# Strided attention scores for two batches in one product, and an attention stage ordered by a list scheduler

## The chip, the core and the metric

The kernel runs on one core of a Trainium2 chip. A core has a matrix engine (TensorE: PE in the profile, its weight loads PEld), a vector engine (VectorE, DVE), a scalar engine (ScalarE, ACT), GpSimd (POOL) and SyncE (SP), which here issues all transfers between HBM and SBUF. Each engine works through its own instructions in their order; a wait holds back all that stands behind it on that engine. The metric is the device time in microseconds (us), lower is better.

## The reference

Three layers, all in 32-bit floats, B = 4 batches, 8 heads, S = 576 positions, D = 64.

```python
# attention: heads 0-3 local (a window of 32), heads 4-7 strided (same position mod 32)
scores = (q @ k.T) / sqrt(64)
mask_local   = (rel >= 0) & (rel < 32)            # rel = query position - key position
mask_strided = (rel >= 0) & (key % 32 == query % 32)
attn = softmax(where(mask, scores, -1e9));  x = attn @ v     # x: 2304 tokens x 512
# soft mixture of experts: 32 slots, 8 experts of 512 x 1024 x 512
logits = x @ phi;  d = softmax(logits, axis=tokens);  c = softmax(logits, axis=slots)
slot_out[e] = relu((d.T @ x)[e] @ w1[e]) @ w2[e];  y = c @ slot_out
# MLP: 512 -> 2048 -> 512 on 2304 tokens
out = elu(y @ w_in) @ w_out
```

## The kernel before, in words

**Stages.** Attention with the pooled slot input runs until about 106 us of the profiled execution, the experts (w1, then w2) until about 142 us, and the last MLP takes the rest. Nearly all input passes through one queue on SP: q, k and v (16 MB), w1 and w2 (16.8 MB each) and the MLP's weights. SBUF is full, so that most weight loads go into regions that an earlier stage has to give up first: the dictionary `LOADS` (lines 424 to 436) issues them after given units.

**Units.** Attention is cut into 20 units (line 39, `ORDER`, L for local, S for strided): a pair of heads and a sixth of the positions of the local pairs (12 units), or a quarter of the residues of the strided pairs (8 units). The strided positions are sorted by residue mod 32, so that one residue has 18 positions (`MR`). One unit passes through these steps:

- `emit_A` (line 165). Local: a mask product (line 172) and 12 products of 32 queries of one batch with 128 key columns (line 180). Strided: a mask product (line 190) and 32 products of 18 queries of one batch with the 18 keys of each of the pair's two heads, 36 columns (line 194); the four batches write four bands of 32 partitions. Each 32-bit product is two passes with a weight load each in the trace. Then on DVE the row maximum (line 205) and the subtraction (line 206), both straight from PSUM.
- `emit_E` (line 212): exp on ACT.
- `emit_N` (line 216): on DVE sum (223), + 1e-9 (224), reciprocal (225), the product with it (229) and a 32x32 transpose (233). `spread` copies the four 32-row bands into a block-diagonal tile `bd`, of which there are two: local units two on ACT and two on GpSimd (lines 241, 243), strided units all four on ACT.
- `emit_PV` (line 253): the product with v (lines 262, 276) and its copy to `x_all` by ACT (lines 267, 281).
- `emit_X` (line 287), after a third of a pair's positions: the product with phi (291), six transposes (298), their copies by ACT (308), the sum into `logits` on DVE (301, 303). There are 12 of these.

**Order.** It is written out by hand in the loop of lines 442 to 457. Iteration `it` issues on DVE the first four steps of unit it-1, then maximum and subtraction of unit it, then the transpose of unit it-1; on PE the scores of unit it, then the product with v of unit it-2, then the `emit_X` that `X_AT` names; on ACT exp of unit it, the spreads of unit it-1, the copies of unit it-2 and those of `emit_X`. The tail (lines 504 to 530) is written out too: the pooled sums `acc` of the three thirds are put between the last units' steps.

```python
    for it in range(nu):
        m = it - 2
        na = emit_N(it - 1) if 0 <= it - 1 < nu else []
        aa = emit_A(it) if it < nu else []
        for f in na[0:4] + aa + na[4:]:
            f()
        emit_E(it)
        for f in pend_S:
            f()
        if 0 <= m < nu:
            emit_PV(m)
        for x in X_AT.get(it, ()):
            emit_X(*x)
        for f in LOADS.get(it, ()):
            f() if callable(f) else f[0](*f[1:])
```

Before the loop, GpSimd builds the masks and clears tiles (lines 314 to 358): the padded key tiles kA and kB, `bd` and `pst`. The experts' stage (lines 577 to 706) and the MLP, whose operations a list scheduler puts in order (lines 985 to 1036), are the same in both kernels.

Of the kernel before, what the change touches and what calls it, by code (L numbers as in the profile page):

```python
# [19 lines left out]
def attn_moe_mlp(ctx, tc, q, k, v_l, v_s, phi, w1, w2, w_in, w_out, out):  # L20
# [18 lines left out]
    ORDER = "LLSLSSLSSLSSLSLLLLLL"  # L39
# [35 lines left out]

    def slot(i, name):
# [21 lines left out]
    smask = misc.tile([128, 1, MR], F32, name="smask")  # L98
# [26 lines left out]
    v2_sb, v3_sb = region("v2", "v2"), region("v3", "v3")  # L125
    VT = {2: v2_sb, 3: v3_sb, 0: v0_sb[:, 0:QW], 1: v0_sb[:, QW:2 * QW]}
# [21 lines left out]
    pend_S = []  # L148

# [7 lines left out]
    nth = [sum(y[0] // 2 == x[0] // 2 for y in units[:n]) for n, x in enumerate(units)]  # L157
    st = {}

# [5 lines left out]
    def emit_A(n):  # L165
        p, t, h = units[n]
        qt, kt = qk_t[p]
        if p < 2:
            u = 2 * t + h
            ps = s_ps[n % 2][:, 0:384].rearrange("p (a b) -> p a b", b=64)  # L170
            m0 = 0 if u == 0 else 1
            nc.tensor.matmul(
                s_ps[n % 2][:, 0:384], ident16, lmask16[:, m0:m0 + 3].rearrange("p i h x -> p (i h x)"),
                start=True, stop=False,
            )
            for j in range(3):
                i = 3 * u + j
                for b in range(B):
                    c0 = 128 * i + 32 * b
                    nc.tensor.matmul(  # L180
                        ps[32 * b:32 * b + 32, 2 * j:2 * j + 2, :], qt[:, c0:c0 + 32], kpair(p, i, b),
                        start=False, stop=(j == 2),
                    )
            s = small("s", 384, "ls", 3, 6, 64)
            ops_ = []
            w = 6
            pa = s
        else:
            ps = s_ps[n % 2][:, 0:16 * MR].rearrange("p (a b) -> p a b", b=MR)
            nc.tensor.matmul(s_ps[n % 2][:, 0:16 * MR], ident16, smask16, start=True, stop=False)  # L190
            for j in range(0, 16, 2):
                for b in range(B):
                    c0 = 576 * h + 288 * (j // 8) + B * MR * (j % 8 // 2) + b * MR
                    nc.tensor.matmul(
                        ps[32 * b:32 * b + MR, j:j + 2, :], qt[:, 1152 * t + c0:1152 * t + c0 + MR], kt[:, t, :, c0:c0 + MR],
                        start=False, stop=(j == 14),
                    )
            s = small("s", 16 * MR, "ss", 3, 16, MR)
            ops_ = []
            w = 16  # L200
            pa = pst[nth[n] % 2][:, :, 0:MR]
        sh = [128, w, s.shape[2]]
        mx = sl_p.tile([128, 16, 1], F32, tag="mx", name="mx", bufs=3)
        sc = ps
        ops_.append(lambda: nc.vector.reduce_max(out=mx[:, 0:w, 0], in_=sc, axis=AX.X))  # L205
        ops_.append(lambda: nc.vector.tensor_tensor(  # L206
            out=s, in0=sc, in1=mx[:, 0:w].to_broadcast(sh), op=ALU.subtract
        ))
        st[n] = [pa, w, sh, s]
        return ops_  # L210

    def emit_E(n):
        pa, s = st[n][0], st[n].pop()
        nc.scalar.activation(out=pa, in_=s, func=AF.Exp, scale=scale)

    def emit_N(n):
        p, t, h = units[n]
        pa, w, sh = st[n]
        sm = sl_p.tile([128, 16, 1], F32, tag="sm", name="sm", bufs=4)
        st[n].append(sm)  # L220
        sv = sm[:, 0:w]
        ops_ = [
            lambda: nc.vector.reduce_sum(out=sv[:, :, 0], in_=pa, axis=AX.X),
            lambda: nc.vector.tensor_scalar(out=sv, in0=sv, scalar1=1e-9, scalar2=None, op0=ALU.add),
            lambda: nc.vector.reciprocal(out=sv, in_=sv),
        ]
        bd = bds[n % 2]
        st[n].append(bd)
        ops_.append(lambda: nc.vector.tensor_tensor(out=pa, in0=pa, in1=sv.to_broadcast(sh), op=ALU.mult))
        r, x = (12, 32) if p < 2 else (16, MR)  # L230
        tr = small("pt", 32 * r, "tr", 2, r, 32)
        pin = pa.rearrange("p a (k x) -> p (a k) x", x=32) if p < 2 else pst[nth[n] % 2]
        ops_.append(lambda: nc.vector.transpose(out=tr, in_=pin))  # L233

        def spread():
            for b in range(B):
                q32 = slice(32 * b, 32 * b + 32)
                o, i = bd[q32, 0:r, 32 * b:32 * b + x], tr[q32, :, 0:x]
                e = SPREAD[1 if p >= 2 else 2 if n == nu - 1 else 0][b]
                if e == "A":  # L240
                    nc.scalar.activation(out=o, in_=i, func=AF.Copy)  # L241
                elif e == "G":
                    nc.gpsimd.tensor_copy(out=o, in_=i)  # L243
                else:
                    nc.vector.tensor_copy(out=o, in_=i)

        pend_S.append(spread)
        return ops_

    SPREAD = ("GAGA", "AAAA", "GAVA")  # L250
    nu = len(units)

    def emit_PV(n):
        p, t, h = units[n]
        pa, w, sh, sm, pt = st.pop(n)
        if p < 2:
            o = o_ps[nth[n] % 2][:, 0:384].rearrange("p (j x) -> p j x", x=128)
            for j in range(3):
                i = 3 * (2 * t + h) + j
                for k in range(2):  # L260
                    for e in range(2):
                        nc.tensor.matmul(  # L262
                            o[64 * e:64 * e + 64, j, :], v_t[p][:, max(i - 1 + k, 0), e, :], pt[:, 4 * j + 2 * e + k],
                            start=(k == 0), stop=(k == 1),
                        )
            i = 3 * (2 * t + h)
            nc.scalar.activation(out=x_all[:, POS[p], i:i + 3, :], in_=o, func=AF.Copy)
        else:
            xv = x_all[:, POS[p]].rearrange("p m (b q) -> p q b m", b=B)
            for g in range(2):  # L270
                og = ps_t.tile([128, 512], F32, tag="t", name="so")[:, 0:4 * B * MR]
                for j in range(4):
                    c0 = B * MR * j
                    r = 4 * g + j
                    for hh in range(2):
                        nc.tensor.matmul(
                            og[64 * hh:64 * hh + 64, c0:c0 + B * MR], v_t[p][:, t, h, hh, r, :],
                            pt[:, 8 * hh + r].rearrange("p (b m) -> p b m", b=B)[:, :, 0:MR], start=True, stop=True,
                        )
                q0 = 16 * t + 8 * h + 4 * g  # L280
                nc.scalar.activation(
                    out=xv[:, q0:q0 + 4], in_=og.rearrange("p (j b m) -> p j b m", b=B, m=MR), func=AF.Copy
                )

    seen = set()

    def emit_X(p, t):
        xt = x_all[:, POS[p], 6 * t:6 * t + 6, :]
        lg = ps_l.tile([128, 192], F32, tag="l", name="lg")
        for b in range(B):  # L290
            nc.tensor.matmul(
                lg[32 * b:32 * b + 32, :], phi_sb[:, p, :], xt[:, :, 32 * b:32 * b + 32], start=True, stop=True
            )
        xps = []
        for g in range(2):
            xps.append(ps_t.tile([128, 3, 128], F32, tag="t", name="xtps"))
            for j in range(3):
                nc.tensor.transpose(xps[g][:, j, :], xt[:, 3 * g + j, :], ident)  # L298
        d = logits[:, 192 * t:192 * t + 192]
        if t not in seen:  # L300
            nc.vector.tensor_copy(out=d, in_=lg)
        else:
            nc.vector.tensor_tensor(out=d, in0=lg, in1=d, op=ALU.add)
        seen.add(t)
        if p == 1:
            nc.vector.reduce_max(out=nm3[:, t:t + 1], in_=d, axis=AX.X)
        for g in range(2):
            nc.scalar.activation(out=xt[:, 3 * g:3 * g + 3], in_=xps[g], func=AF.Copy)

    with tc.manual_schedule():  # L310
# [15 lines left out]
        for b in range(B):  # L326
# [115 lines left out]
        for it in range(nu):  # L442
# [6 lines left out]
            for f in pend_S:  # L449
                f()  # L450
# [636 lines left out]
```

## Time and profile before

| | us |
|---|---|
| median of 3 runs (lowest to highest) | 375.57 (374.45 to 375.98) |
| the profiled execution's own time | 374.55 |
| its span, first to last instruction | 372.8 |
| PE, DVE, ACT, POOL busy | 344.3, 262.7, 246.0, 25.9 |

The profile shows one execution. Its views are the page (shares of each engine, 40 slices of the span with the granted PE clock and the rate of the transfers), groups of instructions, waits (what an idle engine waited for), the chain of waits that ended last, stretches of time, and a timeline.

### The profile page before, as it was taken

To read this page: it belongs to the slowest core of one execution; us is meant where nothing else is said; L and a number is where in the kernel's file an instruction comes from. 1 tells how busy PE (TensorE), PEld (TensorE's weight loads), DVE (VectorE), ACT (ScalarE), POOL (GpSimd) and SP (SyncE) were. 2 spreads that over 40 slices of the span, in tenths; PEclk is the share of its full clock that TensorE was granted. 3 is DMA by queue.
4 is the path that set the end of the run, shared out by engine and by line. 5 is a ranking of instruction groups with operands and counts; after the bars stand their busy time and mean duration, and the time that the engine had idled before them with its cause. 6 is when DMAs were issued, how large, how long until landed. Compare 5 with 4: busy or idle time off the path is not lost.

```text
span 372.8 us, 7425 instructions
## 1 busy us (share of the span) xinstructions
PE 344.3 (92%) x2957; PEld 252.9 (68%) x2957; DVE 262.7 (70%) x535; ACT 246.0 (66%) x482; POOL 25.9 (7%) x60
## 2 busy tenths in 40 slices
PE   7576797798799999999999999999999999999995
PEld 4464565576333337878688778888868888888884
DVE  6778648689261317979999999999854665476741
ACT  5469569767423226999999678868665666666660
POOL 8611011122020000000000000000000000000000
PEclk9699889999999999999999999999999999999999
DMA  7999998996899999755000144100000011033301
GB/s 223 389 414 415 421 419 293 401 413 219 329 413 396 421 408 405 280 225 193 34 1 0 41 186 183 44 1 0 2 0 1 2 56 56 2 113 113 114 0 56
DMA packets 15970, 71.58 MB, mean 192 GB/s; under 512 B 1600, under 2 KB 1856, under 8 KB 11328
## 3 DMA queue, kind: packets, MB, share of 16 engines
q1 hardware_dynamic: 15936, 71.11, 48.9%
q8 instruction: 23, 0.38, 0.4%
q14 instruction: 11, 0.09, 0.1%
HBM read 66.39 MB, written 4.72 MB: 191 GB/s over the span
## 4 chain that ended last, share of the span: by engine, by line
PE 82%; DVE 7%; ACT 4%; POOL 3%; issue 2%; POOLq 0%; ACTq 0%; DVEq 0%
PE ops L939 18%; PE ops L940 18%; PE ops L941 18%; PE hps L897 5%; PE o_ps L671 4%; PE s_ps L581 4%; PE o_ps L262 3%; ACT bd L241 2%; PE xtps L298 2%; PE s_ps L180 2%; DVE tr L233 1%; PE wps L1034 1%; DVE mx L205 1%; PE mps L806 1%; DVE ls L206 1%
## 5 line engine op out<-in xcount | busy, mean ns | idle before, releaser
L907 DVE SCALAR_TENSOR_TENSOR g<-hps,g 128x512 f32<-128x512 f32 (+1 forms) x80 | 50.7, 635 | 19.5 <-ACT g L904 19.4
L901 ACT ACTIVATE g<-hps 128x512 f32<-128x512 f32 (+1 forms) x80 | 44.4, 555 | 20.9 <-PE hps L897 19.4
L904 ACT ACTIVATE g<-g 128x512 f32<-128x512 f32 (+1 forms) x80 | 47.1, 588 | 1.4
L941 PE MATMUL ops<-wh,glo 128*128 128x512 f32 x86 | 33.5, 390 | 0.0
L941 PE MATMUL ops<-w,glo 128*128 128x512 f32 x86 | 33.5, 389 | 0.0
L913 ACT ACTIVATE ghi<-g 128x512 fp32r<-128x512 f32 (+1 forms) x40 | 23.6, 590 | 14.3 <-DVE g L907 12.9
L913 ACT ACTIVATE rings<-g 128x512 fp32r<-128x512 f32 (+1 forms) x40 | 23.5, 588 | 12.4 <-DVE g L907 10.3
L897 PE MATMUL hps<-pers 128*128 128x512 f32 (+1 forms) x80 | 29.3, 372 | 0.0
L939 PE MATMUL ops<-wh,ghi 128*128 128x512 f32 x72 | 28.9, 401 | 0.0
L939 PE MATMUL ops<-wh,rings 128*128 128x512 f32 x72 | 28.8, 400 | 0.0
L241 ACT ACTIVATE bd<-tr 32x288 f32<-32x288 f32 (+1 forms) x56 | 26.8, 479 | 2.7 <-DVE tr L233 1.2
L939 PE MATMUL ops<-w,ghi 128*128 128x512 f32 x72 | 28.5, 395 | 0.0
L940 PE MATMUL ops<-wl,ghi 128*128 128x512 f32 x72 | 28.1, 390 | 0.0
L940 PE MATMUL ops<-w,rings 128*128 128x512 f32 x72 | 28.1, 390 | 0.0
L939 PE MATMUL ops<-w,rings 128*128 128x512 f32 x72 | 28.1, 390 | 0.0
L940 PE MATMUL ops<-w,ghi 128*128 128x512 f32 x72 | 28.1, 390 | 0.0
L940 PE MATMUL ops<-wl,rings 128*128 128x512 f32 x72 | 28.0, 390 | 0.0
L941 PE MATMUL ops<-wh,rings 128*128 128x512 f32 x58 | 22.6, 390 | 0.0
L941 PE MATMUL ops<-w,rings 128*128 128x512 f32 x58 | 22.6, 389 | 0.0
L262 PE MATMUL o_ps<-bd,v 128*64 128x128 f32 x288 | 21.0, 302 | 1.7 <-POOL bd L243 1.7
L262 PEld LDWEIGHTS o_ps<-bd,v 128*64 128x64 f32 x288 | 17.8, 151 | 4.2 <-issue 2.2
L917 DVE TENSOR_TENSOR glo<-g,rings 128x512 fp32r<-128x512 f32 (+1 forms) x24 | 15.2, 634 | 7.2 <-ACT rings L913 4.3
(207 smaller groups left out, 717.9 us busy)
## 6 DMA issues: line engine op xcount, KB each, us to landing
w<-in_moe_w_dram SPq DMA_DIRECT2D x8, 1024.0 KB, 12.2
v<-in_moe_w_dram SPq DMA_DIRECT2D x7, 1024.0 KB, 14.1
w<-in_moe_w_in_dram SPq DMA_DIRECT2D x3, 2048.0 KB, 7.4
out_dram<-ob SPq DMA_DIRECT2D x18, 256.0 KB, 2.0
v<-in_v_s_dram SPq DMA_DIRECT2D x4, 1024.0 KB, 9.8
kB<-in_moe_w_dram SPq DMA_DIRECT2D x4, 1024.0 KB, 12.6
xw<-in_moe_w_dram SPq DMA_DIRECT2D x4, 1024.0 KB, 7.6
xw<-in_moe_w_out_dram SPq DMA_DIRECT2D x2, 2048.0 KB, 7.6
```

The lines of the kernel that those rows point to most:

```text
L241: nc.scalar.activation(out=o, in_=i, func=AF.Copy)
L262: nc.tensor.matmul(o[64 * e:64 * e + 64, j, :], v_t[p][:, max(i - 1 + k, 0), e, :], pt[:, 4 * j + 2 * e + k], start=(k == 0), stop=(k == 1),)
L581: nc.tensor.matmul(hp[32 * g:32 * g + 32, :], siT[:, c, :], w_at(2 * a + g // 2, 0, 2 * c + g % 2), start=(c == CO[0]), stop=(c == CO[-1]),)
L897: nc.tensor.matmul(t["ps"], M4[:, 128 * f:128 * f + 128], cTf[:, t0:t0 + n], start=True, stop=True)
L901: nc.scalar.activation(out=t["g"], in_=t["ps"], func=AF.Exp)
L904: nc.scalar.activation(out=t["g"], in_=t["g"], func=AF.Relu, scale=-1.0, bias=1.0)
L907: nc.vector.scalar_tensor_tensor(out=t["g"], in0=t["ps"], scalar=0.0, in1=t["g"], op0=ALU.max, op1=ALU.subtract)
L913: nc.scalar.activation(out=t["hi"], in_=t["g"], func=AF.Copy)
L917: nc.vector.tensor_tensor(out=t["lo"], in0=t["g"], in1=t["hi"].bitcast(F32), op=ALU.subtract)
L939: nc.tensor.matmul(o, t["hi"][:, c], hi, start=(f == f0), stop=False)
L940: nc.tensor.matmul(o, t["hi"][:, c], lo, start=False, stop=False)
L941: nc.tensor.matmul(o, t["lo"][:, c], hi, start=False, stop=(f == f1 - 1))
```

## The change

Attention is written anew as a list of nodes (engine, duration, dependencies, key, function, buffer), and the scheduler that ordered the MLP is moved into a function, `list_order`, and used for both. For each step the scheduler takes, over all engines, the ready node with the smallest start, and among those of one engine within `AE` of the first the smallest key. A unit n has the key `T0 + TP * n` and its steps offsets from it. New in the function: pools named in `FIFO` give their buffers out in the order of the keys, and PE's nodes carry a count of instructions, which the function charges in blocks of 256, 6.25 us apart.

The strided scores change: GpSimd copies a unit's q to a tile with a pitch of 32 (`f_qw`, into the upper half of region `ex`); a product then takes 64 rows of weights (two batches) and 72 columns (two batches' keys for both heads), 16 products per unit in two halves of 8 that each have a mask product and a PSUM buffer of their own. A row now has its own batch's scores and the other batch's, masked off; `f_cb` takes the larger of the two into SBUF, and maximum and subtraction read that. The product with the reciprocal of the strided units moves to GpSimd. The order of units, the order of the loads and some memsets change too: the first half of kB is cleared by ACT, and GpSimd also clears the q tile. The second half of w1 of expert 1, whose region holds the q tile, now waits for the strided scores. Spreads of the first two units are all on ACT.

```diff
-    ORDER = "LLSLSSLSSLSSLSLLLLLL"
+    ORDER = "LLSLSLSSLSSLSLSLLLLL"
+    RECG, MULG = False, True
+    FIFO = ("sp", "s", "pst", "mx", "sm", "tr", "bd", "o", "qw", "t", "l")
+    T0, TP, AE = 6.0, 2.4, 0.02
...
+    ex_sb = region("ex", "ex")
+    qw = [ex_sb[:, 2048 + 1024 * i:3072 + 1024 * i].rearrange("p (j b x) -> p j b x", b=B, x=32) for i in range(2)]
...
-        nc.gpsimd.memset(smask, 0.0)
+        nc.gpsimd.memset(smask, NEG)
         for b in range(B):
-            sm_ = smask[32 * b:32 * b + 32, 0, :]
+            sm_ = smask[32 * b:32 * b + 32, b % 2, :]
+            nc.gpsimd.memset(sm_, 0.0)
...
-        for e in range(2):
-            nc.gpsimd.memset(kz[1][:, 0, e], 0.0)
+        nc.gpsimd.memset(ex_sb[:, 2048:4096], 0.0)
         nc.gpsimd.memset(bd_slot[:, 2048:4096], 0.0)
...
-        for h, x in ((0, A0), (1, 0)):
+        for i, h, x in ((0, 0, A0), (0, 1, 0), (1, 0, 0)):
             for e in range(2):
                 nc.scalar.activation(
-                    out=kz[0][:, h, e, x:HW_], in_=zero.to_broadcast([128, HW_ - x]), func=AF.Copy,
+                    out=kz[i][:, h, e, x:HW_], in_=zero.to_broadcast([128, HW_ - x]), func=AF.Copy,
                 )
...
+        apools = {
+            "sp": (2, []), "s": (3, []), "pst": (2, []), "mx": (3, []), "sm": (4, []), "tr": (2, []),
+            "bd": (2, []), "o": (2, []), "qw": (2, []), "t": (3, []), "l": (1, []),
+        }
...
+        WS = ((0, 0, ()), (2, 1, v_of(2)), (3, 7, q_of(3)), (4, 5, q_of(3, 0)), (5, 2, v_of(3)))
+        for (a, b), after in ((LO, ()), (HI, q_of(2, 3))):
+            w_node(1, 1, 8, a, b, after)
+        for e, s, after in WS:
+            for a, b in (LO, HI):
+                w_node(e, e, s, a, b, after)
+        for a, b in (LO, (2048, 3072), (3072, 4096)):
+            w_node(6, 6, 6, a, b, v01_of(a, b))
+        for a, b in (LO, HI):
+            w_node(7, 7, 9, a, b, k1_of(a, b))
...
+        for a, b in (LO, HI):
+            w_node(9, 0, 4, a, b, v_of(0, 1, 2, 3), 1)
...
+            def f_qw():
...
+                nc.gpsimd.tensor_copy(
+                    out=z["q"][:, :, :, 0:MR], in_=qt[:, a:a + 576].rearrange("p (j b m) -> p j b m", b=B, m=MR)
+                )
...
+            def f_qks(hh):
...
+                    nc.tensor.matmul(ps, ident16, smask16, start=True, stop=False)
+                    for j in range(4):
+                        for y in range(2):
+                            c0 = 576 * h + 288 * hh + B * MR * j + 2 * MR * y
+                            nc.tensor.matmul(
+                                ps[64 * y:64 * y + 64, 4 * MR * j:4 * MR * j + 4 * MR],
+                                z["q"][:, 4 * hh + j, 2 * y:2 * y + 2].rearrange("p b x -> p (b x)"),
+                                kt[:, t, :, c0:c0 + 2 * MR], start=False, stop=(j == 3),
+                            )
...
+            def f_cb(hh):
...
+                    nc.vector.reduce_max(
+                        out=z["s"][:, 8 * hh:8 * hh + 8], in_=z["sc", hh].rearrange("p r y m -> p r m y"), axis=AX.X
+                    )
...
+            if local:
+                y = an("P", 1.1, deps, K, f_qk, ("sp", rel["sp"]), 50)
...
+            else:
...
+                qs = an("G", 0.85, qd, K - 2.0, f_qw, ("qw", rel["qw"]))
...
+                for hh in range(2):
...
+                    y = an("P", 0.8, deps, K + 0.7 * hh, f_qks(hh), ("sp", r), 34)
...
+                    y = an("V", 0.43, [y] + cb, K + 0.9 + 0.7 * hh, f_cb(hh), None if hh else ("s", rel["s"]))
...
+                y = an("V", 0.36, cb, K + 1.8, f_mx, ("mx", rel["mx"]))
+                y = an("V", 0.38, [y], K + 2.1, f_sub)
...
+            y = an(*(("G", 0.95) if MULG and not local else ("V", c(0.48, 0.45))), [y], K + 3.8, f_mul)
...
+        order, end = list_order(anodes, apools, AE, dict(A=4.8, V=5.2, G=11.0, P=5.0, S=2.0), (256, 6.25, count, 99), FIFO)
+        for t, n in order:
+            anodes[n][4]()
```

## Rows read from the trace of the kernel before

**Rows 1.** The page: transfers in 40 slices of 9.3 us, GB/s.

```profile
GB/s 223 389 414 415 421 419 293 401 413 219 329 413 396 421 408 405 280 225 193 34 1 0 41 186 183 44 1 0 2 0 1 2 56 56 2 113 113 114 0 56
```

**Rows 2.** Busy time by stretch: length, PE, PEld, DVE, ACT, POOL, clock, DMA share, GB/s.

```profile
15.00:97.00 82.00, 65.64 (x1414) 48.79 (x1414) 58.85 (x152) 58.30 (x124) 10.60 (x21) 0.94 0.95 376
106.00:142.00 36.00, 35.90 (x312) 13.17 (x312) 10.93 (x30) 10.26 (x21) 1.89 (x3) 1.00 1.01 407
```

**Rows 3.** Waits of PE, 15 to 97 us: total, times, longest.

```profile
PE xtps L298 <- ACT xw L281: 5.1, 4, 2.4
PE so L276 <- ACT bd L241: 5.0, 5, 1.4
PE s_ps L194 <- issue: 2.8, 2, 2.6
...
PE acc L500 <- DVE d_loc L495: 1.5, 1, 1.5
PE lg L291 <- ACT xw L267: 1.1, 1, 1.1
```

**Rows 4.** Timeline, PE at full clock: one local unit with its emit_X; start, duration.

```profile
77.23 0.33 PE L172 MATMUL s_ps<-lmask,ident 128*128 128x384 bf16 x1
...
78.28 1.53 PE L262 MATMUL o_ps<-bd,v 128*64 128x128 f32 x24
...
79.74 0.53 PE L291 MATMUL lg<-xw,phi 128*32 128x192 f32 x8
...
80.92 0.33 PE L172 MATMUL s_ps<-lmask,ident 128*128 128x384 bf16 x1
```

**Rows 5.** Timeline, PE at full clock: strided scores, and a strided product with v.

```profile
20.38 0.30 PE L190 MATMUL s_ps<-smask,ident 128*128 128x288 bf16 x1
...
20.60 0.75 PE L194 MATMUL s_ps<-kB,q 128*18 128x36 f32 x64
...
22.77 1.22 PE L276 MATMUL so<-bd,v 128*64 128x72 f32 x32 [1.42 <-ACT bd L241]
```

**Rows 6.** Busy time in three stretches in which PE's clock was low; columns of rows 2.

```profile
12.00:18.50 6.50, 4.74 (x105) 3.94 (x109) 4.95 (x13) 3.56 (x7) 3.57 (x10) 0.53 1.00 407
38.00:42.00 4.00, 3.63 (x51) 2.92 (x55) 2.77 (x7) 1.91 (x5) 0.00 (x0) 0.58 1.02 421
48.00:52.00 4.00, 4.00 (x108) 2.94 (x100) 2.09 (x5) 2.67 (x7) 1.00 (x2) 0.61 1.02 419
```

**Rows 7.** Groups on DVE, 15 to 97 us, strided shapes: busy, mean ns.

```profile
L229 DVE TENSOR_TENSOR pst<-pst,sm 128x288 f32<-128x288 f32 x8 | 3.7, 458 | 0.3
...
L205 DVE TENSOR_REDUCE mx<-s_ps 128x16 f32<-128x288 f32 x7 | 3.2, 455 | 6.0 <-PE s_ps L194 6.0
```

**Rows 8.** Timeline of the start: the first strided scores, and one product on DVE.

```profile
12.10 1.17 PE L194 MATMUL s_ps<-kB,q 128*18 128x36 f32 x64 [2.72 <-POOL negm L356]
...
13.95 0.56 DVE L229 TENSOR_TENSOR ls<-ls,sm 128x384 f32<-128x384 f32 x1
```

**Rows 9.** The chain, 13 to 18 us: start, duration, what.

```profile
13.59 0.50 POOL bd L243
14.13 0.76 POOL bd L243
14.93 2.83 PE o_ps L262 x24
```

**Rows 10.** A stretch in which the transfers slackened, and the next; columns of rows 2.

```profile
56.00:66.00 10.00, 7.65 (x198) 5.58 (x196) 7.52 (x20) 9.41 (x20) 1.00 (x2) 1.00 0.87 298
66.00:80.00 14.00, 11.79 (x227) 8.68 (x216) 11.23 (x26) 9.45 (x20) 1.99 (x4) 1.00 1.01 412
```

**Rows 11.** The last piece of w2: issue (123.9 us) and landing; the product that uses it, on the chain.

```profile
L415 SPq DMA_DIRECT2D q<-in_moe_w_dram x1: 327/327/327, 123.9 to 123.9; - x1
...
DMA to landing us min/median/max: 15.4/15.4/15.4
...
138.38 2.07 PE o_ps L671 x16
```

More of the change, by code (lines that the diff above doesn't have):

```diff
@@ L163, in kpair @@
         return bass.AP(tensor=x.tensor, offset=x.offset, ap=[x.ap[0], [QW // 2, 2], [at[1] - at[0], 2], [1, 32]])
[L165 to L248, printed above, removed]
@@ L285, in attn_moe_mlp @@
[L285 to L308, printed above, removed]
+    nu = len(units)
@@ new lines, in users, with load_node @@
+        def users(p, kind, a, b):
+            return [n for n in of[p] if lo_hi[n][kind][0] < b and lo_hi[n][kind][1] > a]
+        qk, pv, data = {}, {}, []
+        RATE = 2.42
+        post = []
+        def load_node(kind, p, a, b, after=()):
+            f = {"q": load_q, "k": load_k, "v": load_v}[kind]
+            need = min(users(p, kind, a, b))
+            key = T[need] - (14 if kind != "v" else 9)
+            dur = 128 * 4 * (b - a) / 1e6 * RATE
+            post.append((key, dur, after, lambda: f(p, a, b), (kind, p, a, b)))
@@ new lines, in attn_moe_mlp @@
+        for kind in "qk":
+            load_node(kind, 0, 0, A0)
+        load_node("v", 0, 0, A0)
+        load_node("q", 0, A0, QW)
+        load_node("k", 0, A0, HW_)
+        load_node("k", 0, HW_, QW)
+        load_node("v", 0, A0, QW)
+        for p in (2, 3):
+            for x in range(2):
+                h = (HW_ * x, HW_ * x + HW_)
+                load_node("q", p, *h)
+                load_node("k", p, *h, after=[("qk", n) for n in users(2, "k", *h)] if p == 3 else ())
+                load_node("v", p, 2048 * x, 2048 * x + 2048)
@@ new lines, in attn_moe_mlp, with make_loads @@
+        made, evs = set(), {}
+        def make_loads():
+            for i, (key, dur, after, f, what) in enumerate(post):
+                if i not in made and all(x[1] in qk and x[1] in pv for x in after):
+                    made.add(i)
+                    deps = [y for k, n in after for y in (qk if k == "qk" else pv)[n]]
+                    y = an("S", dur, deps, key, f)
+                    if what:
+                        data.append((y, what))
+        left = {p: {t: [n for n in of[p] if p >= 2 or units[n][1] == t] for t in range(3)} for p in range(4)}
@@ new lines, in attn_moe_mlp @@
+        for n, (p, t, h) in enumerate(units):
+            make_loads()
+            evs[n] = unit_nodes(n)
+            if n == max(of[3]):
+                rm = an("V", 0.2, [y for m in of[2] + of[3] for y in qk[m]], T[n] + 30, lambda: nc.vector.tensor_scalar(
+                    out=rmask, in0=e0, scalar1=-1.0, scalar2=-NEG, op0=ALU.add, op1=ALU.mult
+                ))
+            for x in range(3):
+                if left[p][x] and left[p][x][-1] == n:
+                    x_nodes(p, x, [y for m in left[p][x] for y in evs[m]], T[n] + 8.5 + (0 if p < 2 else 2.4 * x))
```

505 lines of the change are left out of this document (350 added, 155 removed).

## The prediction

> **What bounds the kernel now.** I read the transfers by slice first, then busy time by stretch, then PE's waits in attention, then the timeline for what a unit costs when nothing holds it up. A measurement of this kernel tells a change from none at about 0.5%, 1.9 us of 375.57.
>
> From 106 to 142 us PE is busy for 35.90 of 36 us [rows 2]: the experts follow attention without a hole, so what attention gains is kept there, if the weights come in time. They hardly do: the last piece of w2, issued at 123.9, lands 15.4 us later, at 139.3, and the product that uses the region started at 138.38 and took 2.07 us [rows 11]. Transfers and PE reach the end of this stage together. The stream moved 389 to 421 GB/s in slices 2 to 15 (to 140 us), but only 293, 219 and 329 in slices 7, 10 and 11 [rows 1]; against 412 [rows 10] these lack (119 + 193 + 83) x 9.32 / 412 = 8.9 us. That is the most the whole kernel can gain before w2 holds it up, apart from the first slices.
>
> In attention no engine is full. From 15 to 97 us (the product of the last unit with v ends at 96.8) PE is busy 65.64, DVE 58.85 and ACT 58.30 of 82 us [rows 2]. PE waits in turn for ACT's copies of x (5.1 and 1.1 us), for ACT's spread (5.0), for the sum's transpose on DVE (1.5) and for its own instructions ("issue", 2.8, of which 2.6 at once) [rows 3]: the fixed order makes each unit's stages wait for one another.
>
> PE's busy time flatters, as part of it is at half clock. At full clock a local unit's scores take 78.28 - 77.23 = 1.05 us, its product with v 79.74 - 78.28 = 1.46, an emit_X 80.92 - 79.74 = 1.18 [rows 4]. Strided scores end 0.97 us after their start, the product with v takes about 1.15 net of overlap with its successor, of 1.22 [rows 5]. So 12 x 2.51 + 8 x 2.12 + 12 x 1.18 = 61.2 us for all units, and some 58.4 of it between 15 and 97 (less the first three units' scores and the last emit_X, plus 1.4 for the pooled sums put in between). The clock was 0.53, 0.58 and 0.61 in three stretches [rows 6], the lower level of 1.2 GHz for most of them, after PE had stood still or nearly so. From 15 on these cost about 1.7 us each, 5 in all. The first unit's product with v shows it: 2.83 us [rows 9] against 1.46.
>
> **The change, step by step, from 15 us to the end of the last product with v.**
>
> *Strided scores.* Before: a mask of 0.22 us and 64 passes in 0.75 [rows 5], 11.7 ns a pass. After: two masks, and 2 x 16 passes with 64 weight columns and 72 moving ones. Exactly this shape stands in the trace, the strided product with v: 32 passes in 1.22, net 1.15 [rows 5], 36 ns a pass. A unit then takes 2 x (0.22 + 0.575) = 1.6 us against 0.97, +0.63, for eight units **+5.0**. Bounds: 0, if half the passes took half the time, and +6.7, if mask and product do not overlap at all. I take the row of the same shape.
>
> A rule speaks against it too. The Trainium skill, page TensorEngine Tiling (Array Packing), section Performance Considerations, says a stationary side of at most 32 columns lets four column tiles work at once, one of at most 64 only two. By that alone 64 x 36 / 4 columns become 32 x 72 / 2, twice the streaming: 0.75 would become 1.5, an estimate, and the term would be +8.0 rather than 5.0. The row of the product with v is cheaper than that, 1.22.
>
> *PE's instructions.* A strided unit's scores issue 130 of them before (64 passes with a weight load each, and the mask's two), 68 after. Where PE stood 2.6 us for issue was inside such a product [rows 3]. I take **-2.3**; bounds 0 and -2.8.
>
> *The first strided unit.* Its scores started at 12.10, held by GpSimd's work of the start [rows 8]. Now GpSimd has another memset of 2048 columns and must copy q after all of it. The nearest row is a copy of 384 columns in 0.50 [rows 9], so 576 take about 0.75. This puts these scores (0.97 us of PE before) behind 15 us, and the pool that gives PSUM buffers out in key order keeps the fourth unit's scores behind them: **+1.0**; bounds 0 and +3.
>
> *DVE.* A strided unit gets two combining maxima from PSUM of the size of the old maximum, 0.455 each, and loses the product, 0.458 [rows 7]; maximum and subtraction stay. 8 x 0.45 = 3.6 us more on an engine that would then be busy for over 80% of a shorter stretch. Two thirds of it I charge to PE as new waits: **+2.4**; bounds 0 and +3.6.
>
> *GpSimd.* Eight copies of q and eight products of 288 columns, by the copy's row 0.4 to 0.8 us each (twice for two inputs), 12 us at most on an engine busy 10.6 of 82 [rows 2]. Cover: the other units' work; without it the longer way (0.4 us and two hand-overs) would stand in eight units' chains, 4 us, which I put into the slower rival. A GpSimd copy that normally took 0.50 took 0.76 when a DVE product with both inputs in SBUF ran at 13.95 [rows 8, 9]. So 0.26 us for each of 16 new operations is the price of a clash, off PE's path. The Trainium skill's page SBUF — State Buffer, section Who interferes with whom, has the two share a read interface by an exclusive lock, so that DVE could be held as well; the subtraction, which now reads SBUF twice, is then exposed. Held for a whole product eight times, it would be 6 us by the upper figure above, an estimate; no row here shows DVE held.
>
> *The order.* The scheduler may issue scores and spreads of later units while x waits for ACT. PE's waits for ACT sum to 5.1 + 5.0 + 1.1 = 11.2 [rows 3]. Two of each PSUM and `bd` buffer let it run about one unit ahead. I let two thirds go, **-7.5**; bounds 0 and -11.2. The late wait for the sum's transpose (1.5) shrinks by **-1.0**, as the first sum is now placed by its due time. Of the 3.3 us that low clock costs after 18.5 us, three quarters go with the standstills, **-2.5**; bounds 0 and -3.3. The stretch before 18.5 stays, since PE is as idle at the start as before.
>
> *Loads.* The order on SP changes. The second half of w1(1), 1 MB, must wait for the last strided scores (now unit 14 of 0 to 19, before 13). Half of w1(6), also 1 MB, could go ahead of that instead. The hole at 56 to 66 us [rows 10] then stays about as it is, and the later two shrink with the last units. Early, k of pair 2 waits for ACT's memset instead of GpSimd's, with v of the first unit queued behind: under 1 us, hidden until about 14 us, when that unit's spread is done. Cost nothing while the w2 stream stays covered; otherwise it is a rival.
>
> Sum: 5.0 - 2.3 + 1.0 + 2.4 - 7.5 - 1.0 - 2.5 = -4.9. The profiled execution took 374.55 (span 372.8), the median of the runs stands 1.0 above it at 375.57. After: 369.7 on the profiled footing, **370.7** as a median. The last product with v would end at about 92. The 16.8 MB of w2, 41 us at 412 GB/s [rows 10], then land by 134 to 135, as PE needs.
>
> **The rivals.**
>
> *The transfers hold it.* If w1's second half leaves the hole at 56 to 66 longer by its 1 MB (2.5 us) and the late holes stay, the last w2 lands little earlier than 139.3 and the experts' products wait for it, a wait that today is 0.2 us. For it: they meet today [rows 11]. Against: the late holes come from waiting for the last units, which come sooner. Gain 1: 374.5.
>
> *Slower: PE gets more work and no better order.* Place: attention, PE. If only a fifth of the ACT waits go (2.2), the clock gains nothing, the sum's wait stays and the other terms stay: 5.0 + 1.0 + 2.4 - 2.3 - 2.2 = +3.9, 379.5. It decides below 6.1 us removed of the 11.2. For it: three engines would each be loaded for over 60 us, with few buffers, and the strided chain has become longer by two hand-overs. Against: the waits are each for work that other ready operations could cover.
>
> *More than forecast.* All ACT waits and the fetch stall go and DVE is hidden: 5.0 + 1.0 - 2.8 - 11.2 - 1.5 - 3.3 = -12.8, of which the stream allows 8.9: 366.7.
>
> **How the numbers follow.** The forecast 0.45, its own range 367.5 to 373.5; more 0.13; transfers 0.23; slower 0.19. Faster by over 0.5% (below 373.7): the forecast, the larger gain and two fifths of the transfer case, 0.67. Within 0.5%: most of the other three fifths and the weaker part of the slower case, 0.17. Slower (over 377.4): 0.16. The range for 8 in 10 is 365.5 to 378.5: the stream's cap with a little from the first slices below, most of the slower rival above.
>
> **What would show it.** Right: strided scores in two groups of 16 passes, about 0.6 us each; PE's waits for ACT under 4 us between 15 and 92; no issue stall of over 1 us in scores; clock 1.00 after 20 us; first strided scores at 14 to 15 us; last product with v at about 92; PE still over 98% busy through the experts. Wrong: passes of the new scores at 45 ns or more; PE waiting for weights in the experts' products; GpSimd on the chain after 20 us; PE's idle time as large as before with DVE as the releaser.

## The result, and the profile after

The changed kernel takes 370.94 us (median of 4, 369.94 to 372.42) against 375.77 for the kernel before (4 runs, 374.45 to 376.83): ratio 0.9863, 95% interval 0.982 to 0.9907. The forecast was 370.7. The profiled execution took 369.94, its span is 368.2. The number came out, but by luck: the way to it was another one than forecast, in two places that cancel.

The page of the kernel after, transfers in 40 slices (of 9.2 us), answers to [rows 1]:

```profile
GB/s 186 379 414 294 393 422 403 417 414 415 418 424 420 414 402 410 155 182 231 1 0 2 119 109 231 0 0 2 0 1 0 2 59 55 2 115 114 116 0 57
```

The three late holes of the kernel before (293, 219, 329 GB/s) are gone. A new one stands in slice 4 (294), and slice 1 moves 186 instead of 223.

Busy time by stretch, kernel after, columns of rows 2; the first line is attention's, the second the experts':

```profile
15.00:88.00 73.00, 70.26 (x1236) 51.73 (x1236) 60.11 (x165) 63.40 (x133) 19.82 (x35) 0.98 0.99 396
106.00:142.00 36.00, 33.27 (x276) 13.24 (x269) 8.96 (x27) 9.04 (x23) 0.00 (x0) 1.00 1.02 413
```

Against [rows 2], PE is busy 96% of attention instead of 80%, at a granted clock of 0.98 instead of 0.94. In the stretch of the experts it was busy 35.90 of 36 us; now it is 33.27.

PE's waits in the kernel after, first those in 15 to 97 us (total, times, longest), which answer to [rows 3]:

```profile
PE s_ps L380 <- DVE dw L805: 1.4, 1, 1.4
PE lg L700 <- ACT xw L625: 0.8, 1, 0.8
PE so L612 <- ACT bd L586: 0.7, 2, 0.4
...
PE s_ps L495 <- DVE ss L534: 0.3, 1, 0.3
PE so L612 <- ACT xw L721: 0.2, 1, 0.2
PE s_ps L519 <- DVE ls L546: 0.2, 1, 0.2
PE o_ps L599 <- ACT bd L586: 0.2, 1, 0.2
```

The first of these comes after the last product with v. Of the 11.2 us that PE waited for ACT, 1.9 are left; "issue" is gone from the list. Then those in 96 to 160 us, where the kernel before had waits of 0.6 us for ACT and of 0.5 and 0.3 for DVE, and none for a DMA:

```profile
PE o_ps L937 <- DMA kB<-in_moe_w_dram: 2.1, 2, 1.4
PE o_ps L937 <- DMA q<-in_moe_w_dram: 0.5, 2, 0.2
```

The chain that ended last, kernel after, 86 to 137 us (start, duration, what):

```profile
86.36 1.46 PE o_ps L599 x24
...
97.14 3.71 PE s_ps L847 x32
...
102.14 17.32 DMA ex<-in_moe_w_dram
...
119.48 15.46 DMA q<-in_moe_w_dram
...
136.04 0.76 PE wps L295 x6
```

And the same view of the kernel before, at the same places:

```profile
95.31 1.49 PE o_ps L262 x24
...
106.83 7.07 PE s_ps L581 x64
...
138.38 2.07 PE o_ps L671 x16
140.44 0.76 PE wps L365 x6
```

This is the whole account, by this pair of traces. The last product with v ends at 87.82 instead of 96.80: attention gave 9.0 us. The experts' products end, and the next stage's begin (the last line of either fence), at 136.04 instead of 140.44: only 4.4 of them are left. From there to the end of the span it is 232.2 us against 232.4, so nothing behind the experts changed. In between two transfers stand on the chain where only PE stood before: the last piece of w2 lands at 134.94, just 4.3 us earlier than the 139.3 of [rows 11], and PE waits for it.

### The profile page after: what moved, and what is told of

Its sections match the earlier page's. It is cut to its first block, busy times and chain, and to the rows that moved or that the text cites. A ratio compares the mean times of both kernels' runs of the same rounds, so it can differ in the third digit from the quotient of the medians.

```text
span 368.2 us, 6970 instructions
## 1 busy us (share of the span) xinstructions
PE 349.5 (95%) x2709; PEld 254.9 (69%) x2709; DVE 265.2 (72%) x542; ACT 250.8 (68%) x488; POOL 35.0 (10%) x76
## 4 chain that ended last, share of the span: by engine, by line
PE 74%; DMA 9%; ACT 8%; DVE 6%; issue 1%; POOL 1%; SPq 0%; POOLq 0%; ACTq 0%
PE ops L1205 18%; PE ops L1206 18%; PE ops L1207 18%; DMA ex<-in_moe_w_dram 5%; PE hps L1163 5%; ACT bd L586 4%; DMA q<-in_moe_w_dram 4%; PE o_ps L599 3%; PE xtps L709 2%; DVE smask L277 1%; PE so L612 1%; PE wps L1260 1%; PE mps L1072 1%; PE s_ps L847 1%; PE mps L1083 1%
## 5 line engine op out<-in xcount | busy, mean ns | idle before, releaser
L586 ACT ACTIVATE bd<-tr 32x288 f32<-32x288 f32 (+1 forms) x60 | 28.8, 479 | 5.9 <-DVE tr L576 4.7
L1183 DVE TENSOR_TENSOR glo<-g,ghi 128x512 fp32r<-128x512 f32 (+1 forms) x24 | 15.2, 632 | 5.0 <-ACT ghi L1179 2.6
L599 PE MATMUL o_ps<-bd,v 128*64 128x128 f32 x288 | 18.2, 276 | 0.3 <-ACT bd L586 0.2
## 6 DMA issues: line engine op xcount, KB each, us to landing
kB<-in_moe_w_dram SPq DMA_DIRECT2D x4, 1024.0 KB, 16.2
```

Of the source, the lines that this page charges most:

```text
L599: nc.tensor.matmul(o[64 * e:64 * e + 64, j, :], v_t[p][:, max(i - 1 + k, 0), e, :], pt[:, 4 * j + 2 * e + k], start=(k == 0), stop=(k == 1),)
L1183: nc.vector.tensor_tensor(out=t["lo"], in0=t["g"], in1=t["hi"].bitcast(F32), op=ALU.subtract)
```

## The experiments

All ratios are against the kernel before on the same chip. The changed kernel, run again beside the last of them, spreads from 369.3 to 373.7 over its ten runs, so versions that differ from it by a microsecond are not told apart by their times. Two traces of it differ as well, by 2.2 us at the end of attention and by 1.2 us at the end of the experts (last run below), and what one trace shows is no better than that.

**Is it the transfers?** In two kernels one expert's w1 (2 MB of the stream) isn't loaded; its products read what stands in the region from before, so that they cost PE the same. Once in the kernel after:

```
-                w_node(e, e, s, a, b, after)
+                if e != 5:
+                    w_node(e, e, s, a, b, after)
...
+        wsl[5, 0] = w_tile_at(2)[:, 0:4096]
```

> The kernel after without the load of w1 of expert 5 (2 MB, 5 us of the stream; the region keeps the values of v, so that the experts' result changes). Theory T: PE's waits for w2 (about 2.6 us in gaps, more in slow products) go, the experts end after 33.6 us of PE as before the change, at about 131 instead of 136.0, time 366 to 367. Rival R: 370 to 371.

Measured: 367.64 us (366.82 to 368.77), ratio 0.9761 [0.969, 0.9832]. PE waits for no weights between 95 and 160 us, the chain through the experts is PE alone, and they end at 133.58 instead of 136.04, though PE's clock was 0.67 in 92 to 99 us, so that the first 32 products took 0.75 us each and not 0.595. That clock, and a first product with w1 at 98.98 instead of 97.14, are why they end later than the expected 131.

Once in the kernel before, where the load at position 15 of the order by hand is taken out:

```
-            15: ((load_w, 5, 0, 2),),
...
+        wsl[5, 0] = w_tile_at(2)[:, 0:4096]
```

> The kernel before with the same load of w1 of expert 5 left out. PE was busy throughout the experts there, and stream and PE met at the end: theory T expects 0 to 1 us less than 375.8 (375.3), PE being the bound. If the kernel before was bound by the stream too: 371 to 372.

Measured: 376.03 us (10 runs), ratio 0.9999 [0.9958, 1.004]. So 2 MB less are worth nothing before and some 3 us after, as it must be if the change has moved the bound of the experts from PE to the weight stream. The run of the kernel before doesn't show its half of this by itself: the holes took up the room (234, 198 and 302 GB/s in slices 9 to 11), and the last piece of w2, issued at 125.3, lands 15.4 us later, at 140.7, no earlier than with the load. That PE was the bound there rests on its 35.90 busy us of 36 [rows 2] and on the chain above.

**What does each half of the change do alone?** The list scheduler with the old strided scores (64 passes of 18 weight columns in one product; no copy of q, no combining maxima):

```
-                y = an("P", 0.8, deps, K + 0.7 * hh, f_qks(hh), ("sp", r), 34)
+                y = an("P", 1.1, deps, K, f_qk1, ("sp", rel["sp"]), 130)
```

> The kernel after with the strided scores of before in its list (32 products a unit, one PSUM buffer, no copy of q, no combining maxima, w1(1) free to load whole; the product with the reciprocal stays on GpSimd): the scheduler alone. By the forecast's own terms PE has 5.0 us less to do, DVE 7.3 less, PE 496 instructions more. If the price of the new scores was right: the last product with v ends at 83 to 84 instead of 87.8, and as 1 MB more may load before the last strided scores, the last piece of w2 lands about 2.5 us earlier, time 368 to 369. Rival (PE's instruction supply binds once the order is good): PE stands for issue 5 us or more within strided scores, the last product with v ends at 88 or later, time 371 or more.

Measured: 370.51 us (369.15 to 372.42), ratio 0.9838 [0.9779, 0.9898]; span 369.3. The same time as with both, by another way. PE's waits of this kernel, 15 to 98 us, the largest:

```profile
PE s_ps L534 <- issue: 6.8, 3, 3.4
PE s_ps L500 <- DMA kA<-in_k_dram: 3.6, 1, 3.6
PE so L620 <- ACT xw L720: 2.3, 2, 1.4
PE so L620 <- issue: 2.0, 1, 2.0
PE xtps L708 <- issue: 1.0, 1, 1.0
```

And its chain (start, duration, what): the last product with v, and the last with w2:

```profile
92.06 1.46 PE o_ps L607 x24
...
134.39 2.77 PE o_ps L936 x16
```

PE stands 9.8 us for "issue", while nothing that the profile shows holds it, at the small passes of the old scores and at other small products: the mechanism of this run's rival. That it is the supply of PE's own instructions fits the next run, and the changed kernel: with half the instructions in a strided unit's scores it is gone from both lists. Another 3.6 us go to a load of k that comes late. Attention ends at 93.5, so the order alone gives 3.3 us. PE's list has no wait for a DMA in the experts, which end at 137.2; but the last 16 products are booked with 2.77 us instead of 2.07, as the last piece of w2 is just landing (issued at 119.8, landed 16.2 us later), so the stream is close here too. The new scores bring attention a further 5.7 us by the first trace of the changed kernel and 3.5 by the second, of which the stream leaves 1.1 and nothing.

The other half: the new scores in the order by hand of the kernel before (with the copy of q, the combining maxima and the product of strided units as they were placed before).

```
+            nc.gpsimd.tensor_copy(out=z["q"][:, :, :, 0:MR], in_=...)
...
-                        nc.tensor.matmul(ps[32 * b:32 * b + MR, j:j + 2, :], ...)
+                        nc.tensor.matmul(ps[64 * y:64 * y + 64, ...], z["q"][:, 4 * hh + j, 2 * y:2 * y + 2], ...)
```

> The kernel before, its order by hand, with the new strided scores alone: q copied on GpSimd, two halves in the two PSUM buffers of the loop, two combining maxima on DVE, the product with the reciprocal left on DVE, the second half of w1(1) loaded after the last strided scores. By the measured prices: PE +6.2 us (8 x (1.75 - 0.97)), DVE +7 us, a GpSimd copy ahead of each strided unit, less the fetch stall of 2.6 and the slow clock behind it, about 1.7. The halves take both PSUM buffers of the loop, so that neighbours wait for each other. If the scores pay only in a good order: 376 to 384, slower than before. Rival (they pay by themselves, since PE's instructions are the trouble): 371 to 374.

Measured: 385.81 us (385.47 to 387.38), ratio 1.0247 [1.0198, 1.0296], slower than the expected 376 to 384. PE's waits, 15 to 98 us, the two largest:

```profile
PE s_ps L204 <- POOL ex L193: 7.6, 2, 5.3
PE xtps L314 <- ACT xw L297: 6.7, 5, 1.8
```

and its busy time by stretch, columns of rows 2:

```profile
15.00:97.00 82.00, 65.54 (x1115) 50.63 (x1119) 62.76 (x150) 52.89 (x112) 16.89 (x32) 0.89 0.86 337
```

No stall for instructions, but the copies of q now stand in PE's way for 7.6 us (5.3 of it at the start, where GpSimd copies q after all its memsets and the first strided scores start at 18.41), PE's clock falls to 0.89, and the last product with v ends at 108.4, 11.6 us later than before. So the halves don't add: in attention the order gives 3.3, the scores cost 11.6, both together give 9.0. By the waits, the new scores need an order, and a start, in which the copy comes early, and the new order needs scores with fewer instructions; neither was tried by itself.

**DVE at the start.** The timeline of the kernel after shows the cast of the strided mask held on DVE while GpSimd clears three buffers in a row:

```profile
5.95 4.74 DVE L277 CAST smask<-smask 128x288 bf16<-128x288 f32 x1 [1.12 <-POOL smask L273]
5.98 1.81 POOL L281 MEMSET ex<- 128x2048 f32 x1
7.72 1.81 POOL L282 MEMSET bd<- 128x2048 f32 x1
9.46 2.22 POOL L284 MEMSET kB<- 128x1152 f32 x2
10.61 0.54 DVE L541 TENSOR_REDUCE mx<-s_ps 128x6 f32<-128x384 f32 x1
```

In the kernel before the same cast took 1.25 us, beside the first memset of kB (a line of its timeline):

```profile
5.45 1.25 DVE L349 CAST smask<-smask 128x288 bf16<-128x288 f32 x1 [0.62 <-POOL smask L343]
```

And in the second trace of the changed kernel it took 6.20 us, to 12.15, when the fifth memset in a row, that of pst, was just done:

```profile
5.95 6.20 DVE L277 CAST smask<-smask 128x288 bf16<-128x288 f32 x1 [1.12 <-POOL smask L273]
```

The edit moves the cast to GpSimd:

```
-        nc.vector.tensor_copy(
+        nc.gpsimd.tensor_copy(
```

> The kernel after, with the cast of the strided mask to 16 bits on GpSimd instead of DVE. There DVE took 4.74 us for it (1.25 before) while GpSimd cleared tiles, and the first row maximum began at 10.61 us. Theory A (DVE is held by GpSimd's memsets): the cast takes under 1 us on GpSimd, the first maximum begins at 8 to 8.5, the stretch up to the last product with v ends 1.5 to 2.6 us earlier. Rival B (the cast is slow by itself, by its new pattern): it takes 1.5 us or more on GpSimd, the first maximum stays at 10 or later, no gain. Total by the theory that the w2 stream sets the end of the experts: 1 to 2.6 us less than the kernel after, by what the hole at 32 to 36 us in the transfers shrinks; if that hole stays, 0.

Measured: 370.36 us (369.89 to 371.98), ratio 0.9838 [0.9766, 0.9911]: nothing that stands out of the changed kernel's spread. The timeline of this kernel says why:

```profile
5.99 0.42 POOL L277 CAST smask<-smask 128x288 bf16<-128x288 f32 x1
7.33 0.56 DVE L541 TENSOR_REDUCE mx<-s_ps 128x6 f32<-128x384 f32 x1 [2.50 <-PE s_ps L503]
...
9.84 2.06 POOL L284 MEMSET kB<- 128x1152 f32 x2
10.04 2.38 DVE L565 TENSOR_SCALAR sm<-sm 128x6 f32<-128x6 f32 x1
```

The cast takes 0.42 us on GpSimd, and the first maximum comes 3.3 us earlier. Then an operation on 6 columns, which elsewhere takes 0.17, is held for 2.38 us behind the last memsets, and the strided scores still wait for the copy of q, to 15.43 instead of 14.55. The last product with v ends at 88.2, not 1.5 to 2.6 us before 87.8 as expected. The hold is real, but taking the 4.74 us away gains nothing, since the copy of q then decides. A longer hold does cost: in the trace with 6.20 us the chain goes through the cast, PE's clock in 20 to 25 us is 0.74 instead of 1.00, and the last product with v ends 2.2 us later. Of the traces of the list order with the new scores, the six with 4.74 us have that end at 87.5 to 88.6, the two with 6.20 us at 90.05 and 90.28. Why the hold is longer in some executions isn't known.

**Closing the hole in slice 4.** SP's waits in the kernel after, 0 to 100 us, two of them:

```profile
SPq L329 <- PE s_ps L523: 9.2, 1, 9.2
...
SPq L216 <- PE s_ps L523: 6.6, 1, 6.6
```

Each is one wait of SP's queue for strided scores. The 6.6 us are the hole: SP issues a piece of q at 25.26 and the next load, of k, only at 32.34, once the strided scores that read the old k are done; the stream runs dry behind it. The 9.2 us are those before w1(1)'s second half, which needs the last strided scores (to 58.7); they leave no hole. One edit issues the first half of w1(0) ahead of the loads that wait:

```
-                w_node(e, e, s, a, b, after)
+                w_node(-188.0 if (e, a) == (0, 0) else e, e, s, a, b, after)
```

> The kernel after, with the first half of w1(0), 1 MB into a region that is free from the start, issued ahead of the loads of strided pair 3 instead of after them; nothing else moves on the other engines but for the allocation of a few products on PE. Theory T (the stream of weights sets when the experts end): the hole at 32 to 36 us is filled, the last piece of w2 lands 2 to 2.6 us before 135.0, and the time falls by as much, to about 368.5. Rival R (PE sets the end, as the last loads wait for regions that PE frees): the last piece lands within 0.5 us of 135.0, the time stays at 371 within 1.

Measured: 369.45 us (368.43 to 370.85, 6 runs), ratio 0.9789 [0.9706, 0.9872]. Transfers by slice, of the page of its profiled execution (span 369.1):

```profile
GB/s 185 374 420 383 384 315 387 406 418 412 423 418 418 418 402 410 169 203 230 1 0 2 99 128 230 0 0 2 0 1 0 2 57 57 2 115 114 115 0 57
```

Slice 4 is up from 294 to 383, and slice 6 down from 422 to 315: what was sent early is missing later, while SP waits 9.5 us for the last strided scores before it can send more. The hole moved. The last piece of w2 lands at 135.87 in this execution (370.85 us, the slowest of the six), where 2 to 2.6 us before 135.0 were expected. Adding half of w1(6), 0.9 MB, to what goes early, with the second half of w1(1) later in the order:

```
-            w_node(1, 1, 8, a, b, after)
+            w_node(2.7 if a else 1, 1, 8, a, b, after)
...
-        for a, b in (LO, (2048, 3072), (3072, 4096)):
-            w_node(6, 6, 6, a, b, v01_of(a, b))
+        for a, b in ((0, 1792), (1792, 2048), (2048, 3072), (3072, 4096)):
+            w_node(6 if a else -6.0, 6, 6, a, b, v01_of(a, b))
```

> The kernel after with w1(0)'s first half early and 0.9 MB of w1(6) moved ahead of the loads that wait for the last strided scores (which are done at 58.6). Theory T2: all that may be loaded before then is loaded, and from there 29 MB stand in one row at 412 GB/s; what moves ahead of that point comes off the end, what moves within the part before it (as the last kernel's 1 MB did) does not. 0.9 MB is 2.2 us: last piece of w2 lands at 132.5 to 133, time 368.5 to 369. Rival T1 (any hole filled counts): with the hole at 32 to 36 and the 0.9 MB both, 4 to 5 us, to 366.5. Rival R (PE sets the end): 371.

Measured: 369.03 us (367.93 to 370.15), ratio 0.9796 [0.9741, 0.985]. Slices 4 to 6 now show 336, 348 and 331 GB/s. The strided scores are done at 61.1 and the last product with v ends at 90.28, 2.5 us later than in the first trace of the changed kernel. That the weights sent early are the reason isn't shown: the cast on DVE took 6.20 us in this execution too, and the second trace of the changed kernel, which has the same cast, has 60.9 and 90.05 without the edit. The last piece of w2 lands at 135.21, not at 132.5 to 133. By itself no gain that can be shown.

The other side of it is to free regions earlier, with the last strided unit at position 13 instead of 14:

```
-    ORDER = "LLSLSLSSLSSLSLSLLLLL"
+    ORDER = "LLSLSLSSLSSLSSLLLLLL"
```

> The kernel after with the last strided unit one place earlier in the order of units (index 13, as in the kernel before); the order of the loads is the same. T2: the last strided scores are done 2 to 4 us before 58.6, the 29 MB behind them start as much earlier, last piece of w2 at 131.5 to 133, time 367.5 to 369, PE's waits in the experts shrink to under 1 us. T1: no change of the holes before, 371. R: 371, or more if attention's order gets worse.

Measured: 370.33 us (369.18 to 370.41), ratio 0.9831 [0.9772, 0.9889]. The strided scores are done 1.9 us earlier, but the stream is still behind from slices 2 and 4 (330 and 348 GB/s), and the last piece of w2 lands at 134.21 instead of the expected 131.5 to 133. In 97 to 104 us PE's clock was 0.72. Why it fell there isn't settled; the chain to the end goes through the last piece all the same. No gain alone either. Both edits together:

> Both edits: loads moved ahead and the last strided unit earlier. T2: gains add until PE binds, whose experts need 33.6 us after about 97.1, so the experts end at 131 to 132 instead of 136.0, time 366 to 367, no waits for weights in the experts. T1: as the kernel with the loads alone. R: 371.

Measured: **367.66 us** (367.49 to 368.4), ratio 0.9763 [0.9713, 0.9813]; its slowest run is faster than the fastest of the changed kernel (369.32). Its transfers by slice, on the page:

```profile
GB/s 185 351 425 403 404 360 413 423 408 416 417 423 418 415 402 409 205 125 232 0 1 2 163 67 232 0 0 2 0 1 2 0 74 41 2 116 115 116 0 57
```

its busy time in attention, columns of rows 2:

```profile
15.00:88.00 73.00, 70.19 (x1240) 51.87 (x1238) 60.93 (x165) 63.41 (x133) 20.12 (x35) 0.98 1.01 405
```

and the chain that ended last, of the same kernel (start, duration, what):

```profile
86.07 1.46 PE o_ps L599 x24
...
101.85 15.76 DMA ex<-in_moe_w_dram
117.62 15.07 DMA q<-in_moe_w_dram
...
133.79 0.76 PE wps L295 x6
```

PE in attention is as it was (70.19 of 73 us busy, last product with v at 87.53). What changed is the stream, 405 GB/s instead of 396: 9 x 73 / 412 = 1.6 us more of it is through by 88 us, and the last piece lands 2.25 us earlier, with PE's end as much earlier right behind it. The expected 131 to 132 for that end was not reached, and PE still waits 1.4 us for weights. This shows the cause from the other side: with attention as long as it was, a fuller stream moves the end.

One more step fills the first 11 us too, where only 188 GB/s move, by sending part of pair 2's k behind the first loads instead of ahead of the first unit's v:

```
-            key = T[need] - (14 if kind != "v" else 9)
+            key = T[need] - (14 if kind != "v" else 9) + (2.75 if (kind, p, a) == ("k", 2, 0) else 0.0)
```

> The kernel with both edits of the loads and the unit order, and k of the first strided pair issued after v and the rest of q and k of the first local pair instead of before, so that SP does not stand at ACT's clearing of kB with those behind it; the hole in the first 11 us of the transfers (193 GB/s there) shrinks. Theory: every hole counts as long as something waits in the queue when the last strided scores are done. 1 to 3 us less than the kernel with both edits (367.7), to 365 to 367, the bound being PE at about 130.5 for the end of the experts. Rival: k comes later, the first strided scores with it, attention ends later, 367.5 to 369.

Measured: 368.81 us (367.89 to 369.47, 6 runs), ratio 0.9784 [0.9752, 0.9816]. The first 11 us move 256 GB/s, but slices 4 and 6 fall back to 325 and 356, and the last piece lands at 133.87. No gain over the version above; whether k's later place is the reason was not tried. The changed kernel beside it:

> The changed kernel itself once more, on the same chip and against the same runs of the kernel before as the one with the filled start: 370 to 371.5.

Measured: 371.46 us (369.32 to 373.73, 6 runs), ratio 0.9853 [0.9812, 0.9894], as at first. Its trace (371.18 us) is the second of the changed kernel, and the chain in it stands so:

```profile
88.59 1.46 PE o_ps L599 x24
...
121.10 15.07 DMA q<-in_moe_w_dram
...
137.27 0.76 PE wps L295 x6
```

Here attention gave 6.8 us (to 90.05) and the stream took 3.6 of them back: the last piece lands at 136.17, and the experts end 3.2 us earlier than in the kernel before. The account is the same as in the first trace, with other sizes.

## Why the prediction was right in its number, and where it failed

The forecast took 4.9 us off attention and let the experts keep them. Attention gave 9.0, and the stream took 4.6 back (6.8 and 3.6 in the second trace); that the two errors leave the forecast sum is luck. Term by term, as measured in the first trace (mean clocks as a share of the stretch's length):

- *Strided scores, forecast +5.0: mis-sized.* The timeline of the kernel after shows one unit:

```profile
37.86 0.72 PE L523 MATMUL s_ps<-kB,ex 128*64 128x72 f32 x16
38.51 0.30 PE L519 MATMUL s_ps<-smask,ident 128*128 128x288 bf16 x1
38.74 0.72 PE L523 MATMUL s_ps<-kB,ex 128*64 128x72 f32 x16
```

  16 passes take 38.51 - 37.86 = 0.65 us and the mask 0.23: a unit takes 1.76 instead of 0.97, eight units +6.3. That is 41 ns a pass, not the 36 of the product with v, which runs 32 in a row. By the Trainium skill, TensorEngine Tiling (Array Packing), Performance Considerations, the streaming should have doubled from 0.75 to 1.5, the forecast's estimate; it took 1.30, between rule and row. (The forecast's own figures give 8 x (0.44 + 1.5 - 0.97) = +7.8 for that rule, not +8.0.)
- *PE's instructions, -2.3.* The stalls went entirely, -2.8. What the step missed is how much they would have cost the new order: 9.8 us with the old scores. The row it used came from an order with more of other waits; that these hid the rest of the stall is a reading, not tried.
- *First strided unit, +1.0.* Its scores start at 14.55, after 2.36 us for GpSimd's copy, within the forecast 14 to 15. The size of the term wasn't measured by itself.
- *DVE, +2.4: wrong.* The waits on DVE in attention are 0.3 + 0.2 us. DVE is busy 82% of the stretch, as forecast, but the list keeps PE supplied with other units' work.
- *ACT waits, -7.5 of 11.2.* 9.3 went. *The sum's transpose, -1.0:* all 1.5 went.
- *Slow clock, -2.5.* A clock of 0.94 over 82 us is 4.9 us lost, 0.98 over 73 us is 1.5: -3.4, an estimate from the means.
- *Loads, "cost nothing while the w2 stream stays covered": the step that failed.* The text had computed that the stream's holes were worth 8.9 us and took this as the limit to the gain. But it asked only which old holes close, and did not cost the new ones. The hole that SP's wait of 6.6 us leaves in slice 4, (412 - 294) x 9.2 / 412 = 2.6 us, and the slower start, 0.8, come off the 8.9, and about 0.4 for slice 5. That leaves some 5 us, near the 4.3 by which the last piece came earlier. The forecast hole, at 56 to 66, did not stay at all.

The sum of the terms as measured, with +1.0 for the first unit as forecast: 6.3 - 2.8 + 1.0 + 0.5 - 9.3 - 1.5 - 3.4 = -9.2, against the 9.0 by which attention shortened. The near agreement is no proof of the single terms, of which the first unit's and the clock's were not measured by themselves; what the rows give without them is PE's busy time, 65.64 to 70.26 or +4.6, and its idle time, 16.4 to 2.7 or -13.6, together -9.0. So the steps but DVE's were right in kind, and the gains were put too low. The text forecast the last w2 at 134 to 135 and got it (134.94, and 136.17 in the second trace); "as PE needs" was wrong, since PE could have used it some 5 us sooner. What happened is, by its mechanism, the rival *more than forecast* in attention, at -9.0 instead of its -12.8, stopped by a tighter form of *the transfers hold it*; the forecast mechanism, experts kept over 98% busy, did not happen. Its own sign for wrong, PE waiting for weights in the experts' products, did. The slower rival's place exists too: it is the new scores without the new order.

PE's timeline in the experts shows how such a loss looks, and why the list of waits (2.6 us) tells only half of the 5.3 us by which the stretch from the first product with w1 to the end of the experts grew (38.9 from 97.14, against 33.6 from 106.83 before):

```profile
126.97 1.07 PE L937 MATMUL o_ps<-kB,h1T_b 128*32 128x512 f32 x8 [0.61 <-DMA kB<-in_moe_w_dram]
129.48 1.06 PE L937 MATMUL o_ps<-kB,h1T_b 128*32 128x512 f32 x8 [1.45 <-DMA kB<-in_moe_w_dram]
```

Eight matmuls run, then PE stands until the next piece lands. Shorter waits, between the last pieces, are counted as the matmuls' own time: the 16 of the last region are booked with 4.3 us, where the kernel before took 2.1 for them.

## What to carry to other kernels

When an early stage is shortened while a load stream of fixed size runs under it, the gain is capped by the stream's holes, those that the new order opens included: draw up when each region comes free in the new order, and cost the stream by it, before counting the gain. Filling one hole moves it unless the regions behind it come free earlier as well; here the two edits, each without a gain that could be shown, together gave some 3 us (2.4 by the spans of two traces). And parts of a change need not add: test each alone, since a shape that costs PE more time can be what makes a denser order possible. Trace the unchanged version twice before you read an edit's effect out of one trace: here two traces of one kernel differ by 2.2 us in attention.

## What the runs showed of the hardware that was not expected

- DVE can be held for a whole chain of GpSimd memsets: a cast that took 1.25 us before took 4.74 in one execution of the changed kernel and 6.20 in another, and an operation on 6 columns 2.38 instead of 0.17. The forecast said that no row shows DVE held; these do. The Trainium skill, SBUF — State Buffer, section Who interferes with whom, has casts and tensor_scalar contend with GpSimd when they run in a mode of DVE that uses both ports, and the other engine blocked for a whole instruction. The trace agrees that DVE is held, but here for three and for five memsets in a row and not for one.
- A product on DVE with both inputs in SBUF took 0.87 us beside GpSimd's copy of q (13.83 to 15.43), against 0.56 in [rows 8].
- PE stood up to 3.4 us at once for "issue" when small matmuls followed one another without other waits, 9.8 us in one attention; with 62 instructions fewer in each of eight strided units there was no such stall. The profile doesn't show the supply of instructions itself, so the cause is inferred from these numbers.
